# Top-k attention with a SoLU feed-forward layer: one PSUM bank for tails, moments and tail products, and another schedule for weights and token tiles

## The chip, the core and the metric

The kernel runs on one core of one Trainium2 chip. A core has five engines that work from queues of their own and wait for one another through semaphores: the tensor engine (PE, matmuls and the loading of their weights), the vector engine (DVE), the scalar engine (ACT), GpSimd (POOL) and the sync engine (SP), which issues the transfers here. Matmuls write to PSUM, which has eight banks; everything else lies in SBUF. The metric is the time of one execution in microseconds on the device; lower is better.

## What is computed

```python
# q, k, v: (8, 8, 576, 64) float32
scores = scale * np.matmul(q, k.transpose(0, 1, 3, 2))
kth = np.partition(scores, -32, axis=-1)[..., -32:-31]
scores = np.where(scores >= kth, scores, -1e9)
attn = np.exp(scores - scores.max(-1, keepdims=True))
attn = attn / (attn.sum(-1, keepdims=True) + 1e-09)
x = (attn @ v).transpose(0, 2, 1, 3).reshape(4608, 512)

h = x @ w_in                       # w_in (512, 1024), float64 in memory
e = np.exp(h - h.max(-1, keepdims=True))
solu = h * e / (e.sum(-1, keepdims=True) + 1e-09)
ln = (solu - mu) / np.sqrt(var + 1e-06) * g_ln     # mean and variance of solu's rows
return ln @ w_out                  # w_out (1024, 512), float64 in memory
```

Eight batches of eight heads, 576 rows of 64; in each row of scores the 32 largest are kept. The result goes as 4608 tokens through a layer that normalizes between two matrix products.

## The kernel before

**Pairs.** The work is cut into 32 pairs of heads, four pairs to a batch. A pair has nine tiles of scores, each 128 x 576: two heads by four tiles of 128 rows, and one tile with the last 64 rows ("tail") of both heads. The 32nd largest of each row is found with counts. A first threshold comes from the row's mean and spread (`spread`, `first_p`, `first`), `count0` on DVE counts what lies above it, `second` makes a better threshold t1 (line 775), `count1` on ACT counts again (`junka`), `third` makes t2 (lines 792 to 800), `count2` on ACT (`sg`) tells the side of every element, `nearest` on DVE collects the eight nearest elements with a subtraction (`w`, line 836) and a `max` (line 840), `kth` picks one of them, `keep` on DVE masks the exponentials, `norm` on POOL divides, PE transposes, and `attn_v` multiplies with v into `om` (512 rows) and `ot` (the tail). `copy_v` copies both to `xTm` and `xTt`, which collect the four pairs of a batch.

**The front of a pair**, which the change touches. `prep_t` transposes the tails of q and k into a tile `tp_t`; `prep_tc` (ACT, line 617) copies it to `qkT`. `prep_m` transposes the main part of q, then of k (`tp_qk`, line 627); `prep_mc` copies them (ACT, lines 635 and 639, the one of k summing as it copies). `moments` multiplies k with itself into `tp_m` (line 649), `moments_c` copies that to `mom` (ACT, line 656). `spread` multiplies q with it: `y_ps` for the main rows and `y_t` for the tail (line 668). `spread_v` on DVE reads both (`yq` and `mean`, lines 686 and 689), `spread_r` sums (`ss`, line 697), and POOL makes `zs` by a power (line 706), on which `first` (line 716) and then `count0` wait. I call the moment at which line 706 of pair i begins zs i, and the time from one to the next a step.

**Token tiles.** Each batch gives four tiles of 128 tokens, and each second batch a tile of tails. A tile is `mm1` (`h_ps`, 16 matmuls by the profile's count), `hmax` (DVE), `hexp` (ACT), `solu` (DVE), `square` (ACT), `ln` (POOL: `var`, `rstd`, `solu`), eight transposes `tp_ln` in two tiles of four, `copy_ln` (ACT), `mm2` (`o_ps`, 16 matmuls) and `store`.

**Weights.** Both matrices are 64-bit floats. They come in 16 chunks of 128 x 512, which DVE and POOL convert in turn: two DVE instructions (lines 31, 34), three on POOL (37, 40, 43), one on DVE (47), one on POOL (50), one on DVE (52), and for w_out a product with g on POOL. `finish_w` is cut into stages by `yield`, and `weights_step` runs one stage.

**Order.** Nothing loops on the chip: every function is entered in a list with a time (`at`), the list is sorted, and the calls are made in that order; the layer below may then move an instruction a few places on its engine where it judges it ready. Times are in steps of `STEP` = 38.0; pair i's front lies 17.2 to 12 before i * 38, its back in the step after. A program's own engine queues show what order came out; both programs' queues are used below.

**PSUM.** Three pools of two slots fill the eight banks: `ps_big` (two banks a slot: `s_ps`, `y_ps`, `h_ps`), `ps_tp` (one bank: all transposes, and `tp_t`, `tp_m`), `ps_o` (one bank: `om`, `ot`, `o_ps`, `y_t`). A tile waits until the last reader of the slot's earlier tile is done.

Of the kernel before, what the change touches and what calls it, by code (L numbers as in the profile page):

```python
# [8 lines left out]
F32 = mybir.dt.float32  # L9
# [6 lines left out]
P = 128  # L16
# [427 lines left out]
def fast_path(  # L444
# [22 lines left out]
    nc = tc.nc  # L467
    B, H, S, D = q.shape
    NTOK, DM = out.shape
    DFF = moe_w_in.shape[1]  # L470
    NM = 4
    SM = NM * P
    ST = S - SM
    SH = S // 2
    NP = H // 2
# [17 lines left out]
    ps_tp = ctx.enter_context(tc.tile_pool(name="ps_tp", bufs=2, space=PS))  # L493
    ps_o = ctx.enter_context(tc.tile_pool(name="ps_o", bufs=2, space=PS))

    pairs = [(b, hp) for b in range(B) for hp in range(NP)]
    NPAIR = len(pairs)
# [19 lines left out]
    def trunc(ap):  # L517

        return ap.bitcast(BF16)[:, 1::2]
# [4 lines left out]
    w_chunks = []  # L524
# [14 lines left out]
    def load_w(n):  # L539
        dst, src, _ = w_chunks[n]  # L540
        if w_wide:
            w_raw[n] = p2.tile([P, 512], mybir.dt.uint64, tag="lnT", name="w_raw")
            dst = w_raw[n]
        nc.sync.dma_start(out=dst, in_=src)

    def finish_w(n):

        dst, _, c = w_chunks[n]
        if n + 1 < len(w_chunks):
            load_w(n + 1)  # L550
        if w_wide:
            tmp = p2.tile([P, 2, 512], F32, tag="solu", name="w_tmp")
            mi = p1.tile([P, DFF], F32, tag="e", name="w_mi")
            yield from float64_stages(
                nc, dst, w_raw.pop(n), tmp[:, 0, :].bitcast(I32),
                mi[:, 0:512].bitcast(U32), tmp[:, 1, :],
            )
        if c is not None:

            nc.gpsimd.tensor_scalar(  # L560
                out=dst, in0=dst, scalar1=g_col[:, c : c + 1], scalar2=1.0,
                op0=ALU.mult, op1=ALU.mult,
            )

    w_gen = [finish_w(n) for n in range(len(w_chunks))]

    def weights_step(n):
# [36 lines left out]
    def prep_t(i):  # L604

        d = st[i]
        d["qkT"] = p2.tile([P, 2, S], F32, tag="qkT", name="qkT")
        tp = d["tp_t"] = ps_tp.tile([P, NM, P], F32, tag="tp", name="tp_t")
        for n, nm in enumerate("qk"):
            nc.tensor.transpose(  # L610
                tp[:, 0, n * ST : (n + 1) * ST], d[nm + "t"].rearrange("p h d -> p (h d)"),
                ident[0:ST, 0:ST],
            )

    def prep_tc(i):
        d = st[i]
        nc.scalar.copy(  # L617
            out=d["qkT"][:, :, SM:S],
            in_=d["tp_t"][:, 0, 0 : 2 * ST].rearrange("p (n s) -> p n s", n=2),
        )  # L620

    def prep_m(i, nm):
# [19 lines left out]

    def moments(i):
        d = st[i]
        tm = d["tm"] = ps_tp.tile([P, NM * P], F32, tag="tp", name="tp_m")
        for c in range(NM + 1):
            for h in range(2):
                kc = trunc(d["k"][:, 2 * c + h, :] if c < NM else d["kt"][:, h, :])
                nc.tensor.matmul(
                    out=tm[h * D : (h + 1) * D, 0:D], lhsT=kc, rhs=kc,  # L650
                    start=(c == 0), stop=(c == NM),
                )

    def moments_c(i):
        d = st[i]
        nc.scalar.copy(out=d["mom"][:, 0:D], in_=d["tm"][:, 0:D])

    def spread(i):

        d = st[i]  # L660
        y = ps_big.tile([P, 2, 512], F32, tag="big", name="y_ps")
        d["ym"] = y[:, :, 0 : NM * (D + 1)].rearrange("p h (t e) -> p t h e", e=D + 1)
        d["yt"] = ps_o.tile([P, 512], F32, tag="o", name="y_t")[:, 0 : D + 1]
        for t in range(NM + 1):
            for h in range(2):
                hd = slice(h * D, (h + 1) * D)
                qs = slice(SM, S) if t == NM else slice(t * P, (t + 1) * P)
                nc.tensor.matmul(
                    out=d["yt"][h * ST : (h + 1) * ST, :] if t == NM else d["ym"][:, t, h, :],
                    lhsT=trunc(d["qkT"][hd, 0, qs]), rhs=trunc(d["mom"][hd, :]),  # L670
                    start=True, stop=True,
                )
# [381 lines left out]
    STEP = 38.0  # L1054

    def at(time, f, *args):
        todo.append((time, len(todo), f, args))

    def pair_times(i):
        b = i * STEP  # L1060
        at(b - 32, load_qk, i)
        at(b + 1, load_v, i)

        at(b - 17.2, prep_t, i)
        at(b - 17.1, prep_m, i, "q")
        at(b - 16.8, prep_tc, i)
        at(b - 16.5, prep_mc, i, "q")
        at(b - 16.4, prep_m, i, "k")
        at(b - 15.4, prep_mc, i, "k")
        at(b - 15.3, moments, i)  # L1070
        at(b - 14.6, moments_c, i)
        at(b - 14.2, spread, i)
        at(b - 13.2, spread_v, i)
        at(b - 12.4, spread_r, i)
        at(b - 12.0, first_p, i)
        at(b - 6.5, first, i)

        for t in range(NM + 1):
            at(b - 9.6 + 1.6 * t, scores, i, t)
        for j in range(NT):  # L1080
            at(b - 8.4 + 0.8 * j, evac, i, j)
            at(b - 3.5 + 0.77 * j, count0, i, j)
            at(b + 5.0 + 0.77 * j, count1, i, j)
            at(b + 16.0 + 0.77 * j + (2.5 if j > 4 else 0), count2, i, j)
        at(b + 4.0, second, i)
        at(b + 12.6, third, i)

        b += STEP
        for g, t in enumerate((12.0, 14.4, 19.5)):
            at(b + t, exps, i, g)  # L1090
            at(b + 4.9 + 4.26 * g, side, i, g)
            at(b + 28.0 + 2.3 * g, inverse, i, g)
        at(b + 22.6, kth, i)
        for j in range(NT):
            at(b + 5.0 + 1.42 * j, nearest, i, j)
            at(b + 25.5 + 0.75 * j, keep, i, j)
            at(b + 29.0 + 0.9 * j, norm, i, j)
            at(b + 30.4 + 0.9 * j, transpose_p, i, j)
            at(b + 30.9 + 0.9 * j, copy_p, i, j)
        for part, t in enumerate((33.6, 37.2, 38.0)):  # L1100
            at(b + t, transpose_last, i, part)
            at(b + t + 0.6, copy_last, i, part)
        for part, t in enumerate((36.0, 38.4, 40.4)):
            at(b + t, attn_v, i, part)
        at(b + STEP + 8.1, copy_v, i, 1)
        at(b + STEP + 8.9, copy_v, i, 2)

    def token_times(n, x, stores, more=0.0):

        d = {"x": x, "stores": stores}  # L1110
        late = n > NPAIR + 1
        b = (NPAIR + 1) * STEP + 10.0 + 15.0 * (n - NPAIR - 2) if late else n * STEP + more
        at(b + 5.5, mm1, d)
        at(b + 12.8, hmax, d)
        at(b + 14.2, hexp, d)
        at(b + 16.5, solu, d)
        at(b + 20.0, square, d)
        at(b + 21.5, ln, d)
        lt, c = (27.7, 29.0) if late else (25.5, STEP + 12.7 - more / 2)
        for g in range(2):  # L1120
            at(b + lt + 0.3 * g, transpose_ln, d, g)
            at(b + lt + 0.6 + 0.4 * g, copy_ln, d, g)
        at(b + c, mm2, d)
        at(b + c + 7.3, store, d)

    def batch_times(b):
        rows = out[b * S : b * S + SM, :].rearrange("(p t) m -> p t m", t=NM)
        n = NP * (b + 1) + 2
        for t in range(NM):
            token_times(  # L1130
                n + t, lambda t=t: xs["m", b][:, :, t * P : (t + 1) * P],
                [(slice(0, P), rows[:, t, :])],
            )
        if b % 2 == 1:
            last = b == B - 1
            token_times(
                n + NM - (not last), lambda: xs["t", b // 2],
                [
                    (slice(m * ST, (m + 1) * ST), out[bb * S + SM : (bb + 1) * S, :])
                    for m, bb in enumerate((b - 1, b))  # L1140
                ],
                0.0 if last else 14.7,
            )

    at(-10.0, load_g)
    at(-14.0, load_w, 0)
    for n in range(len(w_chunks)):
        for t in (0.0, 5.0, 7.5):
            at(10.0 + STEP / 4 * n + t, weights_step, n)
    for i in range(NPAIR):  # L1150
        pair_times(i)
    for b in range(B):
        batch_times(b)
# [7 lines left out]
    for n, (a, lim, op) in enumerate(  # L1161
# [3 lines left out]
            out=hit, in0=a, scalar1=lim, scalar2=None, op0=op, op1=ALU.add,  # L1165
            accum_out=ok[:, n : n + 1],
        )
    tp = ps_tp.tile([P, NM, P], F32, tag="tp", name="tp_ok")
# [4 lines left out]
        out=bad, in0=n_ok, scalar1=3.0 * P * NPAIR * NT - 0.5, scalar2=None, op0=ALU.is_lt  # L1173
# [44 lines left out]
```

## Time and profile before

| | us |
|---|---|
| median of 3 runs | 1581.07 (1580.51 to 1582.61) |
| the profiled execution | 1580.09 |
| its span, first to last instruction | 1578.2 |
| steps without token work (zs 4 to 5, 5 to 6) | 40.3, 39.4 |
| first step with `mm1` (6 to 7) | 42.7 |
| a plain later step (8 to 9) | 43.1 |
| the step with two `mm1` (13 to 14), and the next | 45.0, 46.9 |
| zs 31 to the end of the span | 187.5 |

A trace of one execution gives every instruction's start and duration, and what ended the idle time before it. The page sums them per engine and line; a chain of waits is followed back from the last instruction, at each step to what released it. Steps are read from the starts of line 706: 23.3, 43.8, 85.0, 161.2, 218.1, 258.4, 297.8, 340.4, 383.7, 426.8 for pairs 0 to 9, then every 43 us with three longer pairs of steps, and 1390.7 for pair 31.

### The profile page before, as it was taken

The page shows a single profiled execution, that of the slowest core. Times are in us where ns is not written, and L with a number is a line of the kernel's source. Part 1 is how long each engine was busy: PE and PEld are TensorE (multiplying, and loading weights), DVE is VectorE, ACT ScalarE, POOL GpSimd, SP SyncE. Part 2 cuts the span into 40 slices and gives each one's busy share as a digit, 9 for nine tenths or more (in the row PEclk, how much of TensorE's full clock was granted, in tenths as well). Part 3 has the DMA queues.
Part 4 walks back from the last instruction along what each step waited for, and adds up shares of the span by engine and source line. Part 5 has one row for each costly group of instructions (what it writes and reads, how often), then busy time and mean ns, then how long its engine had stood idle before and what let it go on. Part 6 is the DMA issues. An engine that isn't in the chain of part 4 may idle for free.

```text
span 1578.2 us, 21450 instructions
## 1 busy us (share of the span) xinstructions
PE 1332.5 (84%) x7043; PEld 751.8 (48%) x7043; DVE 1168.7 (74%) x2976; ACT 1144.2 (72%) x2398; POOL 505.4 (32%) x613
## 2 busy tenths in 40 slices
PE   5461576679989899998898899998989889998997
PEld 3231344445545555555554455555555445554543
DVE  4685878887778888877777788877777778877111
ACT  3574557788878877878887887877888778876322
POOL 5667452222222222222222222312222222323110
PEclk9565766688999999999999999998999999999999
DMA  4211101111110001111111100111011110000000
GB/s 109 69 35 56 56 15 24 24 24 31 31 31 24 23 24 30 31 34 26 31 31 31 31 22 17 31 37 31 24 31 31 31 31 16 23 22 7 14 21 22
DMA packets 101898, 48.67 MB, mean 31 GB/s; under 512 B 86921, under 2 KB 95121, under 8 KB 101777
## 3 DMA queue, kind: packets, MB, share of 16 engines
q1 hardware_dynamic: 101776, 47.21, 11.1%
q8 instruction: 57, 0.93, 0.2%
q14 instruction: 65, 0.52, 0.1%
HBM read 37.75 MB, written 9.44 MB: 30 GB/s over the span
## 4 chain that ended last, share of the span: by engine, by line
DVE 36%; PE 27%; ACT 19%; POOL 11%; issue 6%; DMA 0%; SPq 0%; ACTq 0%; POOLq 0%; DVEq 0%
ACT junka L783 9%; DVE w L836 9%; DVE junkv L760 8%; DVE w L840 8%; PE o_ps L1040 7%; PE h_ps L976 6%; ACT sg L815 4%; PE s_ps L741 4%; POOL zs L706 3%; PE om L952 3%; PE tp_ln L1028 2%; PE tp_p L903 2%; DVE E L877 2%; POOL E L892 2%; POOL w_tmp L43 2%
## 5 line engine op out<-in xcount | busy, mean ns | idle before, releaser
L892 POOL TENSOR_SCALAR E<-E,rden 128x576 f32<-128x576 f32 x288 | 227.4, 805 | 746.9 <-ACT xTt L964 424.3
L741 PE MATMUL s_ps<-qkT 64*128 64x288 f32 (+1 forms) x1280 | 284.5, 504 | 66.2 <-ACT X L752 29.9
L783 ACT ACTIVATE junka<-X,t 128x576 bf16<-128x576 f32 x288 | 220.1, 767 | 107.6 <-DVE t L775 104.5
L752 ACT ACTIVATE X<-s_ps 128x576 f32<-128x576 f32 x288 | 175.1, 649 | 135.3 <-PE s_ps L741 131.3
L1040 PE MATMUL o_ps<-w_out,lnT 128*128 128x512 f32 x576 | 253.1, 593 | 0.6 <-ACT lnT L1035 0.5
L877 DVE SCALAR_TENSOR_TENSOR E<-X,kth,E 128x576 f32<-128x576 f32 x288 | 228.4, 826 | 10.6 <-ACT E L847 6.9
L815 ACT ACTIVATE sg<-X,t 128x576 bf16<-128x576 f32 x288 | 220.0, 767 | 21.9 <-DVE t L800 20.6
L976 PE MATMUL h_ps<-w_in,xTm 128*128 128x512 f32 x512 | 231.0, 601 | 0.0
L836 DVE SCALAR_TENSOR_TENSOR w<-X,al,sg 128x576 f32<-128x576 f32 x288 | 228.1, 811 | 0.0
L741 PEld LDWEIGHTS s_ps<-qkT 64*128 64x128 f32 (+1 forms) x1280 | 160.5, 213 | 139.2 <-ACT X L752 53.5
L760 DVE TENSOR_SCALAR_CACHE_REDUCE junkv<-X,t 128x576 bf16<-128x576 f32 x288 | 222.6, 805 | 0.5 <-ACT X L752 0.5
L840 DVE MAX8 w<-w 128x8 f32<-128x576 f32 x288 | 213.2, 752 | 0.0
L903 PE MATMUL tp_p<-ident,E 128*128 128x128 f32 x1152 | 183.4, 293 | 16.6 <-POOL E L892 13.7
L903 PEld LDWEIGHTS tp_p<-ident,E 128*128 128x128 f32 x1152 | 130.9, 147 | 101.7 <-issue 46.6
L917 ACT COPY PT<-tp_p 128x512 f32<-128x512 f32 x256 | 145.2, 593 | 46.5 <-PE tp_p L903 46.4
L1040 PEld LDWEIGHTS o_ps<-w_out,lnT 128*128 128x128 f32 x576 | 109.2, 190 | 138.7 <-issue 132.5
L847 ACT ACTIVATE E<-X 128x1728 f32<-128x1728 f32 x96 | 158.0, 1646 | 0.7 <-PE tp_pt L923 0.6
L952 PE MATMUL om<-PT,vm 128*64 128x256 f32 x1024 | 146.4, 387 | 0.0
L976 PEld LDWEIGHTS h_ps<-w_in,xTm 128*128 128x128 f32 x512 | 95.0, 191 | 106.8 <-issue 105.2
L627 PE MATMUL tp_qk<-ident,km 128*128 128x128 f32 x128 | 29.6, 372 | 110.7 <-ACT qkT L617 110.7
L824 DVE SCALAR_TENSOR_TENSOR al<-n,tt 128x3 f32<-128x3 f32 x96 | 27.6, 288 | 107.2 <-ACT sg L815 105.8
L985 DVE TENSOR_REDUCE hmax<-h_ps 128x1 f32<-128x1024 f32 x36 | 43.7, 1214 | 72.8 <-PE h_ps L976 72.8
(114 smaller groups left out, 1628.8 us busy)
## 6 DMA issues: line engine op xcount, KB each, us to landing
qm<-in_q_dram SPq DMA_DIRECT2D x32, 256.0 KB, 3.4
km<-in_k_dram SPq DMA_DIRECT2D x32, 256.0 KB, 3.4
vm<-in_v_dram SPq DMA_DIRECT2D x32, 256.0 KB, 2.8
out_dram<-osb SPq DMA_DIRECT2D x32, 256.0 KB, 2.3
w_raw<-in_moe_w_in_dram SPq DMA_DIRECT2D x8, 512.0 KB, 3.8
w_raw<-in_moe_w_out_dram SPq DMA_DIRECT2D x8, 512.0 KB, 3.5
qt<-in_q_dram SPq DMA_DIRECT2D x32, 32.0 KB, 2.2
kt<-in_k_dram SPq DMA_DIRECT2D x32, 32.0 KB, 2.8
```

Of the source, the lines that this page charges most:

```text
L741: nc.tensor.matmul(out=s[:, half, 0:SH], lhsT=qkT[hd, 0, qs], rhs=qkT[hd, 1, half * SH : (half + 1) * SH], start=True, stop=True,)
L760: nc.vector.tensor_scalar(out=junk, in0=x_of(i, j), scalar1=d["t0"][:, j : j + 1], scalar2=None, op0=ALU.is_ge, op1=ALU.add, accum_out=d[" ...
L783: nc.scalar.activation(out=junk, in_=x_of(i, j), func=AF.Sign, scale=-1.0, bias=d["t1"][:, j : j + 1], accum_out=d["n1"][:, j : j + 1],)
L815: nc.scalar.activation(out=d["sg", j], in_=x_of(i, j), func=AF.Sign, scale=-(1.0 + 2.0**-23), bias=d["t2"][:, j : j + 1], accum_out=d["n2" ...
L836: nc.vector.scalar_tensor_tensor(out=w, in0=x_of(i, j), scalar=d["al"][:, j : j + 1], in1=d.pop(("sg", j)), op0=ALU.subtract, op1=ALU.mult,)
L840: nc.vector.max(d["w8"][:, j, :], w)
L877: nc.vector.scalar_tensor_tensor(out=e, in0=x_of(i, j), scalar=d["kth"][:, j : j + 1], in1=e, op0=ALU.is_ge, op1=ALU.mult, accum_out=den_a ...
L892: nc.gpsimd.tensor_scalar(out=e, in0=e, scalar1=st[i]["rden"][:, j : j + 1], scalar2=1.0, op0=ALU.mult, op1=ALU.mult,)
L903: nc.tensor.transpose(tp[:, c, :], p_of(i, j)[:, c * P : (c + 1) * P], ident)
L952: nc.tensor.matmul(out=o[h * D : (h + 1) * D, :], lhsT=vm[:, h, c, :] if c < NM else vt[:, h, :], rhs=rhs[0:ks, c, :], start=(c == 0), sto ...
L976: nc.tensor.matmul(out=h[:, half, :], lhsT=x[:, c, :], rhs=w_in[:, c, half * 512 : (half + 1) * 512], start=(c == 0), stop=(c == NP - 1),)
L1040: nc.tensor.matmul(out=d["o"], lhsT=d["lnT"][:, c, :], rhs=w_out[:, c, :], start=(c == 0), stop=(c == NF - 1),)
```

## The change

Four edits. The tails' transposes, the moments and the tail's product `y_t` get one tile `pre` in `ps_o` in place of two tiles in `ps_tp` and one in `ps_o`; the transposes of k and the moments are entered right behind those of q, and the copy of the tails later. The copies `copy_v` are entered at 42.5 and 43.0 after the step's start instead of 46.1 and 46.9. Token tiles begin one step earlier (step 5 instead of 6), apart from the last five, whose times stay. Weight chunks get times of their own: those of w_in every 20.5 from 20, those of w_out every 22 from 50, each load 8 ahead, instead of one chunk every 9.5 from 10 with its load issued by the chunk before.

```diff
     def finish_w(n):
         dst, _, c = w_chunks[n]
-        if n + 1 < len(w_chunks):
-            load_w(n + 1)
...
     def prep_t(i):
-        tp = d["tp_t"] = ps_tp.tile([P, NM, P], F32, tag="tp", name="tp_t")
+        d["pre"] = ps_o.tile([P, 512], F32, tag="o", name="pre")
         for n, nm in enumerate("qk"):
             nc.tensor.transpose(
-                tp[:, 0, n * ST : (n + 1) * ST], d[nm + "t"].rearrange("p h d -> p (h d)"),
+                d["pre"][:, n * ST : (n + 1) * ST], d[nm + "t"].rearrange("p h d -> p (h d)"),
...
     def prep_tc(i):
-            in_=d["tp_t"][:, 0, 0 : 2 * ST].rearrange("p (n s) -> p n s", n=2),
+            in_=d["pre"][:, 0 : 2 * ST].rearrange("p (n s) -> p n s", n=2),
...
     def moments(i):
-        tm = d["tm"] = ps_tp.tile([P, NM * P], F32, tag="tp", name="tp_m")
+        tm = d["tm"] = d["pre"][:, 2 * ST : 2 * ST + D]
...
     def spread(i):
-        d["yt"] = ps_o.tile([P, 512], F32, tag="o", name="y_t")[:, 0 : D + 1]
+        d["yt"] = d["pre"][:, 4 * D : 5 * D + 1]
...
         at(b - 17.1, prep_m, i, "q")
-        at(b - 16.8, prep_tc, i)
+        at(b - 16.9, prep_m, i, "k")
+        at(b - 16.8, moments, i)
         at(b - 16.5, prep_mc, i, "q")
-        at(b - 16.4, prep_m, i, "k")
+        at(b - 16.0, prep_tc, i)
         at(b - 15.4, prep_mc, i, "k")
-        at(b - 15.3, moments, i)
...
-        at(b + STEP + 8.1, copy_v, i, 1)
-        at(b + STEP + 8.9, copy_v, i, 2)
+        at(b + 42.5, copy_v, i, 1)
+        at(b + 43.0, copy_v, i, 2)
...
     def token_times(n, x, stores, more=0.0):
-        late = n > NPAIR + 1
-        b = (NPAIR + 1) * STEP + 10.0 + 15.0 * (n - NPAIR - 2) if late else n * STEP + more
+        late = n > NPAIR
+        b = (NPAIR + 1) * STEP + 10.0 + 15.0 * (n - NPAIR - 1) if late else n * STEP + more
...
     def batch_times(b):
-        n = NP * (b + 1) + 2
+        n = NP * (b + 1) + 1
...
-    at(-14.0, load_w, 0)
     for n in range(len(w_chunks)):
+        w = 20.0 + 20.5 * n if n < 2 * NP else 50.0 + 22.0 * (n - 2 * NP)
+        at(w - 8.0, load_w, n)
         for t in (0.0, 5.0, 7.5):
-            at(10.0 + STEP / 4 * n + t, weights_step, n)
+            at(w + t, weights_step, n)
```

More of the change, by code (lines that the diff above doesn't have):

```diff
@@ L649, in moments @@
                 nc.tensor.matmul(
-                    out=tm[h * D : (h + 1) * D, 0:D], lhsT=kc, rhs=kc,
+                    out=tm[h * D : (h + 1) * D, :], lhsT=kc, rhs=kc,
                     start=(c == 0), stop=(c == NM),
@@ L655, in moments_c @@
         d = st[i]
-        nc.scalar.copy(out=d["mom"][:, 0:D], in_=d["tm"][:, 0:D])
+        nc.scalar.copy(out=d["mom"][:, 0:D], in_=d["tm"])
     def spread(i):
```

## The prediction

> **What bounds the kernel now.** I read the page's totals and its slices first.
>
> ```profile
> span 1578.2 us, 21450 instructions
> PE 1332.5 (84%) x7043; PEld 751.8 (48%) x7043; DVE 1168.7 (74%) x2976; ACT 1144.2 (72%) x2398; POOL 505.4 (32%) x613
> ...
> POOL 5667452222222222222222222312222222323110
> PEclk9565766688999999999999999998999999999999
> ```
>
> No engine is full over the span; POOL is loaded in the first six slices alone (weights), so the stages differ. Next, busy times in stretches between zs (columns: stretch, its length, busy us of PE, weight loads, DVE, ACT, POOL, granted clock, DMA).
>
> ```profile
> 85.00:161.20 76.20, 33.18 (x184) 20.33 (x183) 55.93 (x135) 41.57 (x93) 56.70 (x48) 0.59 0.18 53
> 161.20:218.10 56.90, 30.85 (x184) 18.93 (x182) 41.98 (x100) 32.59 (x69) 38.24 (x33) 0.65 0.15 42
> 258.40:297.80 39.40, 25.95 (x176) 17.04 (x175) 33.73 (x85) 31.66 (x68) 10.95 (x14) 0.72 0.11 25
> 297.80:340.40 42.60, 33.70 (x197) 20.47 (x198) 35.35 (x91) 34.61 (x73) 11.70 (x16) 0.82 0.10 23
> 383.70:426.80 43.10, 39.63 (x219) 22.56 (x215) 34.73 (x91) 35.00 (x74) 11.75 (x17) 0.90 0.11 28
> 644.00:690.90 46.90, 46.27 (x244) 25.36 (x242) 37.10 (x94) 38.11 (x80) 14.19 (x19) 1.00 0.12 31
> 1478.20:1570.60 92.40, 91.43 (x250) 42.51 (x248) 17.94 (x36) 24.34 (x43) 11.59 (x18) 1.00 0.05 17
> ```
>
> The head (to 258) loses time to conversion; a plain step of 43.1 fills no engine; the step after one with two token tiles, and the last 92 us, are PE's alone (99% busy). For the plain step I read the chain of waits from 383 to 428 (start, length, engine and line):
>
> ```profile
> 383.69 1.80 POOL zs L706
> ...
> 403.92 0.08 DVE t L775
> ...
> 404.08 3.90 ACT junka L783 x10
> ...
> 421.80 0.65 ACT qkT L639 x2
> 422.45 0.14 issue
> 422.58 1.08 PE tp_ln L1028 x4
> 423.67 0.35 PE y_ps L668 x8
> ...
> 425.73 0.68 DVE ss L697
> ```
>
> It is a ring: zs, DVE's counts up to t1 (20.2), ACT to the copy of k (18.5), four `tp_ln`, `y_ps`, DVE, zs again. PE's own timeline of the same place shows the wait that the new bank removes, and its clock:
>
> ```profile
> 416.79 0.66 PE L627 MATMUL tp_qk<-ident,qm 128*128 128x128 f32 x4
> 420.60 1.11 PE L627 MATMUL tp_qk<-ident,km 128*128 128x128 f32 x4 [3.15 <-ACT qkT L617]
> 422.58 1.08 PE L1028 MATMUL tp_ln<-ident,solu 128*128 128x128 f32 x4 [0.32 <-ACT qkT L639]
> 423.60 0.40 PE L668 MATMUL y_ps<-mom,qkT 64*128 64x65 bf16 x8
> ```
>
> The same four transposes last 0.66 before the 3.15 us of idleness and 1.11 after it (0.11 and 0.21 from start to start).
>
> **Part 1, the shared bank and the order on PE.** The wait of k's transposes for the tails' copy goes: 110.7 us in 23 waits in the table of waits. PE idles there for ACT; k's copy on ACT (421.75) follows its predecessor without a gap, so nothing on the ring ends earlier by it: worth 0 by itself. PE's idleness moves behind the moments, ahead of `tp_ln`. Two other places of the ring move in the built queues of a plain step.
>
> (a) Ahead of t1 DVE has eight `max` instead of nine (the ninth, and one small instruction, `far`, follow t1). From start to start `max` is 0.67 (446.25 to 446.92 in the step from 426.8) and `far` 0.08: t1 and all of ACT behind it come 0.75 earlier. The moved work lies in DVE's 0.96 us of idleness before line 792; were that full, it would cost the 0.75 again.
>
> (b) All eight `tp_ln` stand before `y_ps`, not four. The first waits for POOL's `solu`, whose end (422.41) moves with ACT to 421.66, and q's slot, free long before; it no longer waits for k's copy. So 421.72 for the first, eight at 0.24 + 6 x 0.214 in all to the start of the last, 423.24, and the 0.35 from last start to `y_ps` as now (423.25 to 423.60): 423.59 against 423.60. The two cancel: a step of 43.07 again. Bounds: if `solu` doesn't advance, +0.74 a step; if PE's clock stays full (0.11 a transpose), eight take 0.82 to the last start and `y_ps` comes 0.8 earlier.
>
> PE idles ahead of `tp_ln` about as long as now ahead of k (3.15 to 3.99 us in plain steps). In 18 plain steps k's transposes ran at 0.21 in 11, at 0.11 in 6, one changed within. The changed place should be full in about 5 of 18: 16 plain steps x 5/18 x 0.8 = 3.6 us gained.
>
> The Trainium skill, "TensorE: Matmul & The Clock Gate", Part 1, says that the clock halves after at least one idle window of some 3.4 us on a free-running count. The trace disagrees in part: gaps of 3.15 and 3.34 were followed by 0.21. Taken strictly a gap of 3.3 would leave nearly every step at full clock, some 13 us; a chance like the row's 11 of 18 makes 3.6, and I take the row.
>
> **Part 2, copies of om and ot earlier.** `xTm` and `xTt` follow the first `junka` on ACT instead of the fifth and sixth. The sum on ACT is the same. `ot`'s matmuls end 1.4 us or more before that place in plain steps, so no wait. Behind them on ACT are eight `junka`, for which t2 waits: any wait would count in full. The first tile of a batch now starts `mm1` in the step in which its last copy is made: PE waits until 21.2 after zs instead of starting at 18.7; `hmax` then comes 0.3 late, but PE's later idle gap shrinks to 1.3 us, so `tp_ln` should run at full clock: -0.5 in each of three plain steps, -1.5 together. In the PE-bound steps (three pairs of 45.0 + 46.9) six more `tp_ln` before `y_ps` (6 x 0.11) cost 0.3 to 0.4 a pair beyond what other PE work fills: +1. Steps in all: -3.6 - 1.5 + 1 = -4.
>
> **Part 3, token tiles a step earlier.** Steps 5 to 29 become what 6 to 30 were; the 39.4 of step 5 goes, and step 30 becomes like the 42.7 of step 15: +3.4. Behind zs 31 PE's queue is the same to the last `ot` (87.5 us). After it `mm2` goes from seven tiles to six, `mm1` from 43 to 35 instructions of 0.859, `tp_ln` from six to five: 6.87 + 8 x 0.859 + 0.87 = 14.6, and of the 2 us of gaps some 0.8 go with it: -15.4. PE was 99% busy there and the tiles' latency (mm1's end at 1553.7 to `tp_ln` at 1562.1: 8.4) stays covered by what is left between; the last copy of `xTm` lies under the 6.87 of an `mm2`. Without that cover each of five tiles could wait up to 2 us, and the gain would be 5.
>
> **Part 4, weights.** The same 64 DVE conversion instructions; by zs intervals (up to zs 0, then each step) 7, 7, 14, 20, 15, 1 become 5, 9, 14, 18, 12, 6. A price from step 3: (56.9 - 39.4) / 15 = 1.17 each. With one price for all the sum is nil; what counts is how long DVE stands before POOL (48.7 us in 21 waits of over 0.6 before conversion instructions, the longest 7.7). I walked the new queues of DVE and POOL with the durations of the rows (POOL 2.1, 0.65, 2.1, 1.3, 0.8 a chunk; DVE 0.4, 0.4, 0.7, 0.7). For example after zs 4: t1 at 19.4, then `kth` with two conversions between, one of which waits 1.8 for POOL, so line 792 falls at 31.5 and zs 5 at 44 instead of 40.3. The walk gives zs 0, 1, 2, 3, 4, 5 at 18, 42, 84, 155, 208, 252 where they are 23, 44, 85, 161, 218, 258. I take -5, between -11 (the walk and as much again) and +7 (six instructions at 1.17 added to step 4 and nothing saved). The loads move past q's, k's and v's on SP: their landing (3.8) lies under the 8 they are ahead, and DMA is 0.24 busy at most in these stretches.
>
> Sum: 1578.2 - 5 - 4 + 3.4 - 15.4 = 1557.2 of span; with the 1.9 around it 1559.1; the median stands 1.0 above the profiled execution: 1560.
>
> **Rivals.** *The clock holds* where PE idles ahead of `tp_ln`: 16 x 0.8 = 12.8 instead of 3.6, 1551. For it: the gap is no longer than now, when a third stays full. Against: all 18 `tp_ln` groups of plain steps ran at 0.21.
>
> *The head gives no gain but a loss*, two chunks at once on POOL: +12 on the sum, 1572. For it: chunks at 160 and 163.5 overlap; against: POOL is 56.7 of 76.2 at most.
>
> *The tail is latency-bound* once shorter, so that starting earlier does not do what it says: 10 less, 1570. Against: 1.4 us of PE idle in the last 92.
>
> *Slower: the spread queues behind the layer norm.* Four more transposes at 0.214 = 0.86 before `y_ps` in every step, if t1's advance is lost before `solu` (DVE full before line 792, or `square` behind something on ACT): 25 x 0.86 = 21.5 on a sum without the -4: 1564 + 21.5 = 1585.5. It decides from 0.68 a step (17 us over 25), and passes the bound of slower from 0.81. For it: POOL's `solu` is now the only releaser; against: every instruction between t1 and `solu` hangs in one chain that moves as a whole.
>
> **How the numbers follow.** Forecast 0.57, with its own range 1553 to 1570; clock 0.12; head 0.12; tail 0.09; slower 0.10. The first four lie below 1577.9 but for a twelfth of them; half of the last is above 1584.2. Faster by over 0.2% (3.2 us, what a measurement of this kernel can tell): 0.83; within: 0.09; slower: 0.08. The range to 8 in 10 runs from the clock's case to beyond the head's, 1548 to 1577.
>
> **What would show it.** Right: zs 5 near 252; a plain step at 43.1, t1 at 19.4 after zs, eight `tp_ln` of 0.21 ending just before `y_ps`; zs 31 to the last `ot` still 87.5, and 77 from there to the last `o_ps`. Wrong: plain steps at 42.3 (the clock held) or 43.8 (the advance was lost), PE gaps over 1 us in the last stretch, or zs 5 later than 258.

## The result, and the profile after

The changed kernel takes 1591.42 us (median of 4 runs, 1589.84 to 1592.89) where the kernel before takes 1581.09 on the same chip (4 runs): a ratio of 1.0064 with a 95% interval of 1.0046 to 1.0081. It is slower by 0.64%; forecast was 1560.

The page of the profiled execution, totals and two rows of the slices:

```profile
span 1588.7 us, 21480 instructions
PE 1353.6 (85%) x7043; PEld 770.0 (48%) x7043; DVE 1177.6 (74%) x2976; ACT 1145.6 (72%) x2398; POOL 510.4 (32%) x613
...
PEclk9555675889998989989998999989899899989999
```

Busy times between zs (columns as before: stretch, its length, busy us of PE, weight loads, DVE, ACT, POOL, granted clock, DMA):

```profile
1488.70:1581.00 92.30, 90.56 (x315) 44.26 (x313) 14.94 (x30) 27.02 (x49) 9.70 (x15) 1.00 0.04 15
217.40:262.90 45.50, 24.21 (x170) 14.96 (x166) 38.97 (x90) 29.88 (x65) 21.75 (x21) 0.73 0.06 16
262.90:307.30 44.40, 35.07 (x192) 20.97 (x191) 36.05 (x91) 34.44 (x72) 11.80 (x17) 0.77 0.09 21
395.10:438.80 43.70, 40.50 (x216) 23.36 (x215) 34.86 (x91) 35.08 (x75) 12.38 (x16) 0.89 0.11 28
615.30:663.80 48.50, 47.00 (x237) 25.67 (x236) 36.41 (x95) 38.37 (x80) 14.09 (x20) 1.00 0.12 30
```

A plain step (the fourth row) is 43.7 with the same DVE and ACT work in it (34.86 and 35.08, were 34.73 and 35.00). The step after a double one (the fifth) is 48.5, PE busy for 47.0 of it; it was 46.9. Step 4 (the second) is 45.5 where it was 40.3. By stages, in the two profiled executions:

| | before | forecast, change | after | change |
|---|---|---|---|---|
| start to zs 5 | 258.4 | -5 | 262.9 | +4.5 |
| zs 5 to zs 31 | 1132.3 | -0.6 | 1152.7 | +20.4 |
| zs 31 to the end | 187.5 | -15.4 | 173.1 | -14.4 |

The tail did nearly as foreseen. Of the 20.4 in the middle 3.4 come from the shift of the token tiles, as foreseen. The other 17 are spread over the steps: 16 plain ones of 43.47 on the mean against 43.08 (6.3), three groups of a double step, the next and the one after, a group 137.6 long on the mean against 134.6 (9 in all), and the first token step, 44.4 against 42.7 (1.7).

The chain of waits through the plain step from 395 (start, length, engine and line):

```profile
395.10 1.80 POOL zs L705
...
414.83 0.87 ACT junka L782 x2
...
427.79 0.31 DVE solu L999
428.10 0.81 issue
429.27 2.19 POOL E L891 x3
431.55 0.19 POOL var L1015
431.82 0.57 POOL rstd L1019
432.49 1.21 POOL solu L1020
433.74 1.97 PE tp_ln L1027 x8
435.71 0.34 PE y_ps L667 x8
```

It no longer goes through ACT's copies. From DVE's `solu` it goes to POOL, where the three divisions `E` of the pair's third group stand in front of `var`, and from POOL's `solu` to eight `tp_ln` and `y_ps`. PE's timeline of the place:

```profile
429.67 0.60 PE L626 MATMUL tp_qk<-ident,km 128*128 128x128 f32 x4
...
433.74 1.97 PE L1027 MATMUL tp_ln<-ident,solu 128*128 128x128 f32 x8 [3.08 <-POOL solu L1020]
```

The transposes of k follow those of q at 0.11 each, the idleness (3.08) now lies ahead of `tp_ln`, and these run at 0.21: all as forecast. What is wrong is the place. After zs the first `tp_ln` starts at 38.64, where 38.03 was forecast (before: 38.90), and `y_ps` at 40.54 instead of 39.91.

Why POOL is late is seen when its timeline before is laid beside that after. Before:

```profile
409.32 4.72 POOL L892 TENSOR_SCALAR E<-E,rden 128x576 f32<-128x576 f32 x6 [23.54 <-ACT xTt L964]
...
418.01 2.18 POOL L892 TENSOR_SCALAR E<-E,rden 128x576 f32<-128x576 f32 x3 [3.16 <-DVE nmu L1004]
420.28 0.19 POOL L1016 TENSOR_SCALAR var<-var 128x1 f32<-128x1 f32 x1
```

After:

```profile
420.81 5.37 POOL L891 TENSOR_SCALAR E<-E,rden 128x576 f32<-128x576 f32 x6 [23.61 <-DVE rden L887]
...
429.27 2.19 POOL L891 TENSOR_SCALAR E<-E,rden 128x576 f32<-128x576 f32 x3 [2.42 <-DVE nmu L1003]
```

Already before, `var` (420.28) began right at the end of the third group (420.19), not at the end of `square` (419.92, the last instruction of line 1010 on ACT):

```profile
419.73 0.19 ACT L1010 ACTIVATION_READ_ACCUMULATOR e_sb<-solu,nmu 128x1 f32 x1
```

The prediction had not looked at who releases `var`. From zs the third group starts at 34.33 before and 34.17 after, so t1's 0.68 (line 775 at 20.15 and its like at 19.47) shrinks to 0.16 on its way there. Where the rest stays, DVE's timelines show. Before:

```profile
413.98 0.81 DVE L877 SCALAR_TENSOR_TENSOR E<-X,kth,E 128x576 f32<-128x576 f32 x1
...
414.72 0.81 DVE L877 SCALAR_TENSOR_TENSOR E<-X,kth,E 128x576 f32<-128x576 f32 x1
...
416.45 1.28 DVE L1000 SCALAR_TENSOR_TENSOR solu<-h_ps,rs,e_sb 128x1024 f32<-128x1024 f32 x1
...
417.65 0.17 DVE L888 RECIPROCAL rden<-rden 128x3 f32<-128x3 f32 x1
```

After:

```profile
424.76 0.81 DVE L876 SCALAR_TENSOR_TENSOR E<-X,kth,E 128x576 f32<-128x576 f32 x1
...
425.50 1.29 DVE L876 SCALAR_TENSOR_TENSOR E<-X,kth,E 128x576 f32<-128x576 f32 x1
...
427.70 1.28 DVE L999 SCALAR_TENSOR_TENSOR solu<-h_ps,rs,e_sb 128x1024 f32<-128x1024 f32 x1
...
428.91 0.17 DVE L887 RECIPROCAL rden<-rden 128x3 f32<-128x3 f32 x1
```

POOL's third group divides by the result of that reciprocal, which stands behind `solu` in DVE's queue (the profile names `nmu`, the instruction right behind it). DVE begins its third group (`keep`) 0.64 sooner after zs, while POOL's six divisions begin no sooner (25.63 before, 25.71 after), and the two meet: POOL's six take 5.37 instead of 4.72, DVE's second `E` 1.29 instead of 0.81, and DVE's `solu` begins only 0.16 sooner. One `E` of DVE is so stretched in 21 of the 25 steps from 6 to 30, against 1 before. The Trainium skill, "SBUF — State Buffer", section "Who interferes with whom", says that a DVE instruction with two SBUF inputs and a GpSimd instruction that reads SBUF exclude each other, and the second waits for the whole of the first. The trace fits it in kind: POOL's sixth division began 0.04 after DVE's first `E` and took 1.38 instead of 0.74, and DVE's second `E` began while that division still had 0.68 to run and grew by 0.48, less than the whole of it.

### The profile page after: what moved, and what is told of

It reads as the page before. It is cut to its first block, busy times and chain, and to the rows that moved or that the text cites. A ratio compares the mean times of both kernels' runs of the same rounds, so it can differ in the third digit from the quotient of the medians.

```text
span 1588.7 us, 21480 instructions
## 1 busy us (share of the span) xinstructions
PE 1353.6 (85%) x7043; PEld 770.0 (48%) x7043; DVE 1177.6 (74%) x2976; ACT 1145.6 (72%) x2398; POOL 510.4 (32%) x613
## 4 chain that ended last, share of the span: by engine, by line
DVE 37%; PE 29%; ACT 14%; POOL 13%; issue 6%; SPq 0%; DMA 0%; DVEq 0%; POOLq 0%; ACTq 0%
DVE w L835 10%; ACT junka L782 8%; DVE junkv L759 8%; PE o_ps L1039 7%; PE h_ps L975 6%; DVE w L839 6%; PE s_ps L740 4%; DVE E L876 4%; PE om L951 3%; PE tp_ln L1027 3%; POOL zs L705 3%; PE tp_p L902 3%; ACT sg L814 2%; POOL E L891 2%; POOL solu L1020 2%
## 5 line engine op out<-in xcount | busy, mean ns | idle before, releaser
L891 POOL TENSOR_SCALAR E<-E,rden 128x576 f32<-128x576 f32 x288 | 234.2, 832 | 723.2 <-DVE rden L887 648.0
L740 PE MATMUL s_ps<-qkT 64*128 64x288 f32 (+1 forms) x1280 | 314.0, 531 | 68.6 <-ACT X L751 30.2
L740 PEld LDWEIGHTS s_ps<-qkT 64*128 64x128 f32 (+1 forms) x1280 | 175.9, 224 | 149.1 <-ACT X L751 56.9
L876 DVE SCALAR_TENSOR_TENSOR E<-X,kth,E 128x576 f32<-128x576 f32 x288 | 240.3, 868 | 9.5 <-ACT E L846 6.2
L902 PE MATMUL tp_p<-ident,E 128*128 128x128 f32 x1152 | 194.5, 307 | 55.1 <-ACT qkT L634 33.6
L902 PEld LDWEIGHTS tp_p<-ident,E 128*128 128x128 f32 x1152 | 140.5, 155 | 144.8 <-issue 39.3
L1027 PE MATMUL tp_ln<-ident,solu 128*128 128x128 f32 x288 | 55.5, 346 | 87.0 <-POOL solu L1020 87.0
L951 PEld LDWEIGHTS om<-PT,vm 128*64 128x64 f32 x1024 | 74.4, 136 | 46.7 <-issue 18.7
L984 DVE TENSOR_REDUCE hmax<-h_ps 128x1 f32<-128x1024 f32 x36 | 43.7, 1214 | 65.2 <-PE h_ps L975 65.2
## 6 DMA issues: line engine op xcount, KB each, us to landing
qm<-in_q_dram SPq DMA_DIRECT2D x32, 256.0 KB, 3.4
km<-in_k_dram SPq DMA_DIRECT2D x32, 256.0 KB, 3.5
vm<-in_v_dram SPq DMA_DIRECT2D x32, 256.0 KB, 2.8
out_dram<-osb SPq DMA_DIRECT2D x32, 256.0 KB, 2.3
```

What stands on the lines that cost most here:

```text
L740: nc.tensor.matmul(out=s[:, half, 0:SH], lhsT=qkT[hd, 0, qs], rhs=qkT[hd, 1, half * SH : (half + 1) * SH], start=True, stop=True,)
L876: nc.vector.scalar_tensor_tensor(out=e, in0=x_of(i, j), scalar=d["kth"][:, j : j + 1], in1=e, op0=ALU.is_ge, op1=ALU.mult, accum_out=den_a ...
L891: nc.gpsimd.tensor_scalar(out=e, in0=e, scalar1=st[i]["rden"][:, j : j + 1], scalar2=1.0, op0=ALU.mult, op1=ALU.mult,)
L902: nc.tensor.transpose(tp[:, c, :], p_of(i, j)[:, c * P : (c + 1) * P], ident)
L951: nc.tensor.matmul(out=o[h * D : (h + 1) * D, :], lhsT=vm[:, h, c, :] if c < NM else vt[:, h, :], rhs=rhs[0:ks, c, :], start=(c == 0), sto ...
```

## The experiments

Each run stands beside the kernel before on its own chip (medians 1581.74, 1582.95 and 1581.73 in the three groups of four). "Plain" is the mean of the 16 plain steps, "long" the step after a double one.

| run | us | ratio, 95% interval | zs 5 | plain | long | zs 31 to end |
|---|---|---|---|---|---|---|
| before | 1581.09 | 1 | 258.4 | 43.08 | 46.9 | 187.5 |
| changed | 1591.42 | 1.0064 (1.0046 to 1.0081) | 262.9 | 43.47 | 48.5 | 173.1 |
| bank_alone | 1599.13 | 1.0115 (1.0099 to 1.0130) | 261.5 | 43.47 | 48.5 | 186.4 |
| tiles_alone | 1571.54 | 0.9936 (0.9922 to 0.9949) | 258.8 | 43.11 | 46.9 | 174.2 |
| weights_alone | 1581.89 | 1.0002 (0.9993 to 1.0011) | 259.6 | 43.09 | 46.9 | 186.4 |
| no_bank | 1572.68 | 0.9943 (0.9930 to 0.9957) | 259.7 | 43.07 | 46.9 | 173.6 |
| own_moments | 1566.16 | 0.9896 (0.9879 to 0.9912) | 256.0 | 43.01 | 46.8 | 174.0 |
| third_norm_dve | 1568.88 | 0.9913 (0.9896 to 0.9929) | 261.3 | 42.57 | 48.5 | 169.3 |
| own_moments_third_norm_dve | 1564.10 | 0.9882 (0.9865 to 0.9898) | 256.6 | 43.07 | 46.8 | 170.9 |
| pe_kept_busy | 1590.44 | 1.0053 (1.0036 to 1.0070) | 263.4 | 43.55 | 48.5 | 174.1 |
| pe_busy_same_order | 1582.83 | 1.0002 (0.9991 to 1.0013) | 263.1 | 43.15 | 48.5 | 173.3 |
| spread_first | 1576.81 | 0.9971 (0.9958 to 0.9983) | 263.3 | 42.69 | 48.5 | 173.1 |
| shared_bank_in_plain_steps | 1560.16 | 0.9860 (0.9844 to 0.9877) | 255.8 | 42.80 | 46.7 | 169.7 |
| plain_steps_and_pe_busy | 1554.00 | 0.9831 (0.9815 to 0.9848) | 255.9 | 42.48 | 46.7 | 169.8 |

### The parts one by one

**bank_alone**: the hunks of `prep_t`, `prep_tc`, `moments`, `moments_c`, `spread` and the order of the front's entries, on the kernel before.

> The kernel before with the shared PSUM bank and its order of entries alone. Theory A (t1's advance is lost before POOL writes `solu`, so the four extra transposes in front of `y_ps` cost some 0.7 us in each step in which PE runs slow there, and the stalls after double steps come from the same edit): 25 steps, about +14 to +20, 1595 to 1601. Theory B (the steps got longer through the earlier token tiles and copies; the bank edit is neutral, as the prediction had it): 1577 to 1583.

Measured 1599.13, as A has it. Plain and long steps are those of the changed kernel, 43.47 and 48.5. The bank edit costs 17.4.

**tiles_alone**: the hunks of `token_times`, `batch_times` and `copy_v` on the kernel before.

> The kernel before with token tiles a step earlier and the copies of `om` and `ot` earlier (the earlier tiles need them), nothing else. Theory A: the shorter tail (14.4) against the step that becomes a token step (3.4), so about -11, 1568 to 1572. Theory B: the longer steps come along, so -11 + 17 = +6, about 1587.

1571.54: theory A. The steps stay at 43.11 and 46.9, so the earlier tiles and copies lengthen none of them, and B falls.

**weights_alone**: the hunks of `load_w` and `weights_step`.

> The kernel before with the new times of the weight chunks alone. Both theories: the head of the changed kernel reached zs 5 4.5 us late and its step 4 carried six conversion instructions, so +4 to +7, 1585 to 1588. If the walk of the prediction was right and the bank edit spoiled the head: -5, 1576.

1581.89, neither: the new times of the weights are worth nothing by themselves (+1.2 at zs 5). Step 2 became 73.4 from 76.2 and step 3 52.6 from 56.9, but steps 1 and 4 grew to 47.9 and 43.9 from 41.2 and 40.3.

**no_bank**: the other three edits together.

> The changed kernel without the shared bank and its order: weights, copies and token tiles as changed, tails and moments as before. Theory A: -11 of the tiles and +4 to +7 of the weights, 1573 to 1578. Theory B: as the changed kernel, 1589 to 1593.

1572.68, just below A's range. The bank edit is the whole loss: on top of the other three it costs 18.7 (19.4 with each run taken against its own kernel before).

### What in the bank edit costs it

**own_moments**: the changed kernel with the moments in a tile of their own.

```diff
-        tm = d["tm"] = d["pre"][:, 2 * ST : 2 * ST + D]
+        tm = d["tm"] = ps_tp.tile([P, NM * P], F32, tag="tp", name="tp_m")[:, 0:D]
```

> The changed kernel with the moments back in a `tp_m` of their own in `ps_tp`, the tails and `y_t` still sharing a bank; PE's queue has four `tp_ln` before `y_ps` and four behind it again. Theory A (the four extra transposes at 0.21 in front of `y_ps` are the loss): plain steps 43.0, the step after a double one back near 46.9, 1591.4 - 17 = 1572 to 1576. Rival (the shared bank itself slows PE or ACT): plain steps 43.4 to 43.8, 1587 to 1592.

1566.16: the steps are as A has them (43.01 and 46.8), and the time is lower than A's range since the head came along, zs 5 at 256.0 instead of 262.9. This single line turns the change from a loss into a gain of 1.0%. The second `tp_ln` tile now waits for `tp_m` again, so PE's queue has four `tp_ln` ahead of `y_ps`. DVE's queue too is back at nine `max` ahead of t1, with no stretched `E` in steps 6 to 30: the order and the lost advance go together here. The long step shows what seven `tp_ln` ahead of `y_ps` do where PE is the bound. The changed kernel, PE, from 611:

```profile
611.25 1.05 PE L1027 MATMUL tp_ln<-ident,solu 128*128 128x128 f32 x7
612.23 0.31 PE L667 MATMUL y_ps<-mom,qkT 64*128 64x65 bf16 x8
...
619.28 1.43 PE L740 MATMUL s_ps<-qkT 64*128 64x288 f32 x8 [0.54 <-DVE solu L999]
...
622.03 1.78 PE L740 MATMUL s_ps<-qkT 64*128 64x288 f32 x8 [0.75 <-ACT X L751]
```

The same place with the moments' own tile:

```profile
598.53 0.30 PE L1027 MATMUL tp_ln<-ident,solu 128*128 128x128 f32 x1 [0.22 <-ACT qkT L638]
598.77 0.31 PE L667 MATMUL y_ps<-mom,qkT 64*128 64x65 bf16 x8
...
599.15 0.98 PE L1027 MATMUL tp_ln<-ident,solu 128*128 128x128 f32 x7
```

There `y_ps` comes at once and the seven follow it; PE has no idleness over 0.3 in the double step or the next. In the changed kernel PE stands for 0.54 and 0.75 behind DVE and ACT, which got `y_ps` and `s_ps` later, and PE never makes that up in a step that it fills. Idle gaps over 0.1 us come to 1.44 in this step, against 0.67 with the moments' own tile; the difference is somewhat under half of the 1.7 by which the step is longer, and the rest, inside PE's own groups, was not followed.

**third_norm_dve**: the changed kernel with the third group's divisions on DVE, which idles for 3.2 us behind `nmu`.

```diff
-        nc.gpsimd.tensor_scalar(
+        (nc.vector if j > 5 else nc.gpsimd).tensor_scalar(
             out=e, in0=e, scalar1=st[i]["rden"][:, j : j + 1], scalar2=1.0,
```

> The changed kernel with the third group's three divisions `E` on DVE (which idles 3.2 us there) instead of POOL. Theory A (t1's advance of 0.7 is stopped by POOL's third group standing before `var`): `var` follows `square` at 35.7 after zs instead of 36.45, the first `tp_ln` at 37.9 instead of 38.6, plain steps at most 42.9, and 42.2 where the shorter wait leaves PE's clock full: 18 to 25 steps by 0.8 to 1.5, 1560 to 1578. Rival (the advance is lost elsewhere, on ACT or in DVE's own queue): plain steps stay at 43.7, 1589 to 1594.

1568.88, A. POOL's `var` in a plain step is now released by ACT's `square` (`e_sb`):

```profile
427.33 0.19 POOL L1015 TENSOR_SCALAR var<-var 128x1 f32<-128x1 f32 x1 [3.94 <-ACT e_sb L1009]
```

That is 35.67 after zs instead of 36.45, and the first `tp_ln` follows at 37.85. Plain steps are 42.9 where `tp_ln` runs at 0.21 (step 6, behind the first token tile's step, is 43.7), 42.0 to 42.2 where it runs at 0.11, and 42.25 to 42.7 where it begins so and falls; the long step stays at 48.5. Half-rate steps are thus some 0.8 shorter than in the changed kernel, as A has it; the mean falls by 0.90 because more steps ran at the full rate. So POOL's third group is where the advance was held up. That DVE's `E` and POOL's divisions meet is read from the traces and was not tried by itself; the stretched `E` is still there in this run.

**own_moments_third_norm_dve**: both.

> Both edits together, moments in a tile of their own and the third group's divisions on DVE. Theory A: four `tp_ln` begin at 37.9 after zs, `y_ps` waits for `mom` at about 39.0 instead of 39.9, plain steps 42.2: 18 x 0.8 = 14 below the run with the moments' own tile, 1557 to 1563. Rival (ACT's copies set `y_ps` by then, the divisions do not matter): as that run, 1572 to 1576.

1564.10, between the two ranges, and no plain step is shorter (43.07): the rival's reason holds. `tp_ln` (38.87 after zs) waits for ACT's copy of k again, which with nine `max` ahead of t1 ends at 38.7. The 2 us gained lie behind zs 31 (170.9 for 174.0). With ACT's copies where they were before, a sooner POOL brings the steps nothing: two paths end here within some tenths of each other.

### The clock ahead of `tp_ln`

**pe_kept_busy** and **pe_busy_same_order**: transposes that nothing reads, 24 into `pre`, or 12 into a tile of their own, behind the moments in the plain steps.

```diff
     def moments(i):
...
+        if i - 1 in (4, 5, 6, 7, 8, 9, 10, 11, 15, 16, 17, 18, 19, 23, 24, 25, 26, 27):
+            fill = ps_big.tile([P, 2, 512], F32, tag="big", name="fill")
+            for _ in range(12):
+                nc.tensor.transpose(fill[:, 0, 0:P], ident, ident)
```

> The changed kernel with 24 further transposes of `ident` into unread columns of `pre` behind the moments in the 18 plain steps (4 to 11, 15 to 19, 23 to 27), so that PE idles under 0.7 us before `tp_ln` instead of 3.2. Theory A (PE's clock halves in that idleness and the eight `tp_ln` cost 0.85 more for it): all plain steps 42.8 as steps 10, 15, 18 and 25 are now, some 13 x 0.85 = 11 less, 1578 to 1582. Rival (the rate there does not come from the idleness): no change, 1589 to 1593, or more where the added work is in the way.

1590.44, a miss of A, but not through the clock. In step 8, for one, `tp_ln` ran at 0.11 and ended before 39.5 after zs; but ACT's queue had got three `sg` ahead of the copies of `pre`, `mom` was copied at 39.9 instead of 38.7, and `y_ps` waited for it until 40.2. The second run leaves ACT's order alone.

> The changed kernel with 12 further transposes of `ident` into a PSUM tile of their own behind the moments in the 18 plain steps; the orders on PE and ACT are otherwise those of the changed kernel (in the run with 24 into `pre`, ACT's copies of `pre` came three `sg` late). PE's idleness before `tp_ln` falls from 3.2 to about 1.9. Theory A (the half clock comes from that idleness): `tp_ln` at 0.11 in all plain steps, `y_ps` at 39.75 after zs, steps of 42.8: 13 x 0.85 = 11 less, 1578 to 1582. Rival (1.9 of idleness is enough for the half clock, or idleness is not its cause): 0.21 stays, 1589 to 1593.

1582.83 (ten runs, 1577.97 to 1585.06): 8.6 less than the changed kernel, 0.8 short of A's range. In this run the rate goes with the idleness from step to step. Steps 8 and 9 on PE:

```profile
432.68 1.97 PE L1032 MATMUL tp_ln<-ident,solu 128*128 128x128 f32 x8 [4.36 <-POOL solu L1025]
```

```profile
473.85 1.53 PE L656 MATMUL fill<-ident 128*128 128x128 f32 x12
476.37 1.09 PE L1032 MATMUL tp_ln<-ident,solu 128*128 128x128 f32 x8 [0.99 <-POOL solu L1025]
```

In step 8 PE's work ended early and it idled 4.36 in spite of the added transposes; step 8 took 43.7, step 9 42.7. With up to 2.65 of idleness all nine such groups ran at 0.11, with 3.36 to 4.39 five of six at 0.21; the one behind 2.95 fell from 0.11 to 0.21 on the way.

**spread_first**: the same with 24, at which PE's queue has `y_ps` ahead of all eight `tp_ln`.

> The same with 24 transposes, at which PE's queue has `y_ps` ahead of all eight `tp_ln` in the plain steps. Theory A (in the changed kernel `y_ps` is late only for standing behind `tp_ln`): `y_ps` waits for `mom` alone, at 39.0 after zs instead of 40.5, plain steps 42.2: 18 x 1.5 less than 1591.4, 1562 to 1568. Rival (the eight `tp_ln` then hold up `s_ps` and give it back): plain steps 42.8 or more, 1578 or above.

1576.81, between the two. `y_ps` does wait for `mom` alone:

```profile
431.70 0.41 PE L672 MATMUL y_ps<-mom,qkT 64*128 64x65 bf16 x8 [2.53 <-ACT mom L660]
```

But that is 39.65 after zs, not 39.0: in this queue too t1 has nine `max` ahead of it, and ACT copies `mom` at 39.4 instead of 38.7. Plain steps are 42.69, 0.78 less than in the changed kernel, although t1's advance is gone. So the eight `tp_ln` ahead of `y_ps` do cost time there, and the advance of t1 is a term of its own. How much each is worth this run does not part, since the order on PE, the order on DVE and PE's rate all differ in it.

### A version that beats both

**shared_bank_in_plain_steps**: moments in the shared bank in the plain steps alone, a tile of their own elsewhere, third group on DVE.

```diff
-        tm = d["tm"] = d["pre"][:, 2 * ST : 2 * ST + D]
+        tm = d["tm"] = (
+            d["pre"][:, 2 * ST : 2 * ST + D]
+            if i - 1 in (6, 7, 8, 9, 10, 11, 15, 16, 17, 18, 19, 23, 24, 25, 26, 27)
+            else ps_tp.tile([P, NM * P], F32, tag="tp", name="tp_m")[:, 0:D]
+        )
```

> The changed kernel with the moments in the shared bank in the plain steps 6 to 11, 15 to 19 and 23 to 27 alone and in a `tp_m` of their own elsewhere, and the third group's divisions on DVE. Theory A: plain steps 42.5 on the mean as with the divisions moved (42.0 to 42.9), head and longer steps as with the moments' own tile: 1564.1 less 16 x 0.5, 1554 to 1558. Rival (the mixture upsets the order, or the gain of the plain steps is given back in the longer ones): 1562 to 1567.

1560.16, between the two: the long steps keep 46.7 and zs 5 255.8, but plain steps are 42.80, with 43.6 to 43.9 in those that follow a change of tile (6, 15, 23).

**plain_steps_and_pe_busy**: that and the 12 transposes.

> That kernel with 12 further transposes of `ident` in the plain steps. Theory A: all plain steps at 42.0, as where `tp_ln` runs at 0.11 with the divisions moved: another 16 x 0.5 less, 1546 to 1551. Rival (the added work is in the way): as that kernel or slower, 1554 to 1560.

1554.00, at the rival's lower end, though by A's mechanism: nine of the 16 plain steps are 42.0 to 42.1, not all. It is 1.7% faster than the kernel before (0.9831, 0.9815 to 0.9848).

## Why the prediction was wrong

**Part 1, (b), failed: "the first waits for POOL's `solu`, whose end (422.41) moves with ACT to 421.66".** From zs, `solu` moved by 0.14, not 0.75. The prediction carried t1's advance through ACT to `square` and from there to `var`, and took the whole for one chain ("every instruction between t1 and `solu` hangs in one chain that moves as a whole"). In the trace of before `var` is released by POOL's own third group, 0.36 us behind `square`; that group hangs on a reciprocal that stands behind `solu` in DVE's queue, and DVE loses half a microsecond on the way by running into POOL's earlier divisions. The sum for a plain step with half clock is then 4 x 0.214 = 0.86, less the 0.26 by which `tp_ln` starts sooner: 0.60; measured 0.63 in step 8, near the prediction's own bound of +0.74 for a `solu` that does not advance. Its sign for a lost advance, plain steps at 43.8, came in the steps at half rate (43.7 to 44.0). This is the mechanism of the rival "the spread queues behind the layer norm", which had 0.10; it named DVE being full and `square`, and POOL was the place.

**The PE-bound steps were mis-sized.** "+1" for six more `tp_ln` in three pairs of steps; measured 6.9 in these pairs, and 2.0 more in the three steps behind them (43.4 for 42.7), in which all eight `tp_ln` ran at 0.21 ahead of `y_ps`. The prediction counted the transposes and not the waits that a later `y_ps` makes: `s_ps` waits for slots that DVE and ACT free later, and a step that PE fills gives none of it back.

**Right in Part 1:** t1 0.68 sooner (0.75 forecast), k's transposes without a wait, the idleness behind the moments, worth 0 by itself. **The clock came out too:** full in 4 of 16 plain steps and for a part of `tp_ln` in 3 more, where 5 of 18 was taken. Those four steps are 42.7 to 42.8. But that chance was carried over from the row of k's transposes, not derived from what makes the clock fall (the last section), so that it fitted is partly luck.

**Part 2's -1.5 did not appear.** In the first token step of a batch the last copied part of `xTm` is needed by a later matmul of `mm1` only. In steps 9, 17 and 25 of the run with tiles alone PE starts `mm1` at 18.3 to 18.7 after zs, as in other steps, and stands for 0.39 ahead of its seventh matmul in step 9; these steps are 43.0 to 43.1.

**Part 3 was right:** tail -14.4 for -15.4, the shift +3.4; with the tiles alone the time falls by 10.2. A gap over 1 us, its sign for a tail that waits, did come: 1.27 ahead of `tp_ln` at 1522.2, where the longest before was 0.49.

**Part 4 failed as a gain of 5, and its range of -11 to +7 holds the +4.5.** The head's terms do not add one by one. Zs 5 moves by +1.2 with the weights alone and by +3.1 with the bank alone; with all four edits it moves by +4.5, and with the moments in a tile of their own, the weight times kept, by -2.4 (zs 0 to 5 are 19.3, 41.4, 85.0, 160.0, 212.0 and 256.0). So the gain of 5 is missing without the bank edit too, and on top of it the moments' bank takes 6.9. About half of these 6.9 can be seen. In the changed kernel the order of DVE's queue puts a conversion between two instructions of `kth` in step 3, and it waits for POOL:

```profile
185.84 0.57 DVE L866 TENSOR_TENSOR kth<-al,zk_all 128x9 f32<-128x9 f32 x1
188.45 0.69 DVE L47 SCALAR_TENSOR_TENSOR w_tmp<-w_raw,w_tmp 128x512 f32<-128x512 uint32 x1 [2.04 <-POOL w_tmp L37]
189.06 0.57 DVE L867 SCALAR_TENSOR_TENSOR kth<-kth 128x9 f32<-128x9 f32 x1
```

With the moments' own tile the same two stand together:

```profile
183.22 0.58 DVE L866 TENSOR_TENSOR kth<-al,zk_all 128x9 f32<-128x9 f32 x1
183.84 0.17 DVE L867 SCALAR_TENSOR_TENSOR kth<-kth 128x9 f32<-128x9 f32 x1
```

Step 3 is 55.3 in the one and 52.0 in the other. A bank for the moments moved DVE's order in the head through the planner. The walk saw the wait in step 4 (line 792 at 31.5; it came at 33.2) and missed this one. Its largest error lies in step 2, 71 by the walk and 75.2 measured (75.0 with the moments' own tile); what it missed there no run shows.

The sum: 6.9 of the head's miss of 9.5 and 18.4 of the steps' miss of 21.0 go away with the moments' own tile (zs 5 at 256.0 instead of 262.9; zs 5 to 31 1134.3 instead of 1152.7). That was one edit, priced at 0 but for the clock's 3.6, in which two opposite terms of 0.75 and 0.86 were to cancel. The cover that made it nothing was an advance that had to pass three engines, and its loss was priced in a rival, with too small a chance.

## What to carry to other kernels

When two terms are to cancel, follow the one that gains through every engine to the place where it is needed, and ask at each instruction in the trace of before who releases it: an instruction that starts at the end of its own engine's previous one is held by that queue, however near the named producer is. Where two paths end within a few tenths of each other, moving one gives nothing, and an edit that lengthens the common part behind both costs in full. A PSUM tile that is freed later also orders the queue; take its wait away and the planner puts other work in front, so compare what stands ahead of the critical instruction, not only what waits.

## What the runs showed of the hardware

The length of PE's idleness alone does not decide its rate. Groups of `tp_ln` behind 2.51 to 2.79 us of idleness ran at 0.11 in the changed kernel (4 of 4), and behind 2.58 to 2.76 at 0.21 in the run with the third group on DVE (5 of 5). What differs is where they fall on a fixed grid: in the profile's record of the granted clock, all changes from full to half and back in these two runs lie whole multiples of 3.41 us apart. Busy time of PE, granted clock and DMA in such windows of the changed kernel, before and behind a fall (step 8, then step 10):

```profile
430.22:433.63 3.41, 0.44 (x11) 1.00 0.36 104
433.63:437.05 3.42, 3.31 (x21) 0.50 0.31 69
518.96:522.37 3.41, 1.39 (x18) 1.00 0.62 163
522.38:525.79 3.41, 3.41 (x12) 0.50 0.29 65
```

In step 8 the fall (433.63) comes right ahead of `tp_ln` (433.74), in step 10 (522.38) only behind all eight. In all nine groups named above the fall lies ahead of those at 0.21 and behind those at 0.11. Between zs 6 and zs 31 of the changed kernel every fall (19) follows a window in which PE's matmuls were busy for at most 0.51 of it, and every window that full clock outlived (258) has at least 0.60; with the third group on DVE it is at most 0.57 (18) and at least 0.60 (258). The ends of matmuls are modelled, and other runs have exceptions, such as a window of 0.43 that full clock outlived in the run with `y_ps` first and a fall behind one of 0.80 in the run with 24 transposes. So these counts are a reading of two traces, and no run varied the share by itself.

The Trainium skill, "TensorE: Matmul & The Clock Gate", Part 1, has the clock halve after at least one idle free-running window of some 3.4 us. The grid of 3.41 agrees with that; the word idle does not, since half clock followed a window in which PE was busy for 1.39 of 3.41 us.

DVE and POOL slow each other where both work on `E` in SBUF (1.29 for 0.81, and 5.37 for 4.72 over six), so that work that comes sooner on one of the two can end no sooner.
